# Another hand-written order of the commands in the likely branch of an attention and maxout kernel

## The chip, the core and the metric

The kernel runs on one core of a Trainium2 chip. The metric is the device time of one execution in microseconds (us). The engines are TensorE (PE in the profile; PEld is its loading of weights), VectorE (DVE), ScalarE (ACT), GpSimd (POOL) and SyncE (SP), which here only issues DMAs.

## What is computed

Attention over 4 batches, 8 heads, 768 positions and 64 features per head. A flag for each head says whether it is a retrieval head (plain causal attention) or a streaming head (causal, and only the first 4 keys and the last 64). The heads' outputs stand side by side as 3072 tokens of 512 features and go through a maxout feed-forward:

```python
scores = q @ k.T / sqrt(D)
scores = where(mask[head], scores, -1e9)   # causal, or causal & (sink | window)
a = softmax(scores)
x = (a @ v).transpose(0, 2, 1, 3).reshape(B * S, H * D)
h = maximum(maximum(x @ w1, x @ w2), x @ w3)
out = h @ w_out
```

## The kernel before

**Tiles.** A batch is cut into two halves of 384 queries; the heads are cut into two groups of four, and a group into two pairs. A "task" t counts batch, half and group: t = 4b + 2·half + group. The feed-forward runs over one half of a batch at a time, in 21 units: 18 maxout units (one of the three weights, one of six blocks of 128 hidden features; four matmuls of 384 columns) and 3 output units (128 tokens, six matmuls of 512 columns against `woutt`). There are eight such halves, and the units run strictly in that order.

**A program of commands.** The schedule is manual: the program order of the instructions on each engine is the order in which commands of a written list are executed when the kernel is built. Each engine works its own instructions off in that order and waits on semaphores where data or a buffer is missing. The flags are read at run time. A first list, FIRST, is common; then the kernel branches: the list NEAR runs where the flags have the pattern that the kernel expects (they have here), ANY otherwise; a last list, REST, is common again, behind two units that are computed ahead. The commands, with a letter at the end for the engine of the copy (d VectorE, a ScalarE, p GpSimd):

- `f 1 e`: the next unit of the feed-forward (L648 matmuls, evicted at L668 and L673; output units L692, evicted at L698 and written by SP at L699). The letter decides only for copies; the maximum is always VectorE's.
- `s t u`: unit u of the scores of task t (matmuls L876), and their exponential on ScalarE (L887). For batch 0 a third number can name one pair alone.
- `k t i u e`: a mask of pair i multiplied onto the exponentials (L908, L926).
- `av t i`: the product with the values (L964), its division (L977, L979); with `D`, SP then issues a DMA that transposes the result into xT (L984), where the feed-forward reads it. Without D, `x t i e` turns it on TensorE (L998) and copies it (L1002).
- `load b g` (GpSimd issues, L389) and `turn b g i part` (VectorE, L407) bring in and transpose keys and queries of batches 1 to 3; `cast` and `turnp half pair ee` do so for batch 0 by TensorE (L362), with one letter for each of two halves.
- `load_v b half` (SP issues, L458) and `v t i e` (L734) load and cast values; for batch 0, `v` and `vp half n e` (L747, L750) put them in order by matmuls. `c` (L799) and `kc` (L784, L790) make joined values and keys, `vf` scaled ones (L762).
- `w n`: GpSimd issues the loads of a weight (L619; `w 3`, the output weights, L623). `after_w` is a small DMA on SP that reads the output weights (L418): SP's queue waits there until they have landed.
- `m`, `nm`, `on`: masks and constants; `gate`: another waiting DMA on SP.

**Buffers that couple the engines.** In PSUM there are two score tiles `st` of two banks each, and four single banks:

```python
    sps = turns("sps", 2, space=bass.MemoryType.PSUM)
    bkp = turns("bkp", 4, space=bass.MemoryType.PSUM)
    ...
        t = bkp.tile([P, 512], FP32, tag="bank", held=False)
```

Both are taken in turn, in the order of the commands. Every unit `f`, every `av`, `x`, `vp` and each of the two halves of a `turnp` takes one `bank`; a matmul into a bank waits until the engine that evicts the bank's last contents has done so.

The list NEAR begins like this:

```python
    "x 0 0 d, w 0 2 1, x 1 1 a, x 0 1 d, cast 1 2 0 d, v 3 1 d, s 2 2 0, s 2 1 0, turnp 1 3 dd",
    "f 1 d, c 0 1 0 d, s 2 1 1, vp 1 1 a, m 0, w 1, turnp 1 2 dd, k 2 0 0 d, f 1 d, turn 1 0 0 0",
```

Of the kernel before, what the change touches and what calls it, by code (L numbers as in the profile page):

```python
# [72 lines left out]
)  # L73

NEAR = (
# [40 lines left out]
)  # L116

ANY = (
# [1029 lines left out]
```

## Time and profile before

| | |
|---|---|
| median of 3 runs | 188.49 us (188.47 to 189.35) |
| the profiled execution | 188.78 us |
| its span, first to last instruction | 187.1 us |
| mean granted TensorE clock | 1.000 |
| busy: TensorE, VectorE, ScalarE, GpSimd | 180.8, 139.9, 103.5, 85.6 us |
| read from HBM, written | 25.17 MB, 6.29 MB |

Busy times are shares of the span. Matmuls are pipelined, so their records overlap: what one costs is read from the distance between the starts, not from its length. Idle time on an engine matters only where somebody that sets the end waits for it.

### The profile page before, as it was taken

Reading aid. Unit: us, or ns where it says so; the run is one execution under the profiler, and the core shown is the slowest. Engines: PE = TensorE matmul, PEld = TensorE weight load, DVE = VectorE, ACT = ScalarE, POOL = GpSimd, SP = SyncE. Lnnn points to the kernel's source line nnn. Section 1 sums busy time; section 2 is a strip of 40 time slices with the busy share of each in tenths; the row PEclk is TensorE's granted clock in tenths of the full one; section 3 lists DMA queues with packets and bytes.
Section 4 is the critical chain, followed back from the end, with each engine's and each line's share of the span. In section 5 each row is a group of like instructions: output and inputs, shape, how many; then the busy total and the mean of one; then the engine's idle time right before and its main releaser. Section 6 shows DMA issues by size and latency. Waiting matters only on the chain. (4 is left out here: it accounts for less than half of the span.)

```text
span 187.1 us, 4937 instructions
## 1 busy us (share of the span) xinstructions
PE 180.8 (97%) x1930; PEld 104.4 (56%) x1930; DVE 139.9 (75%) x297; ACT 103.5 (55%) x164; POOL 85.6 (46%) x121
## 2 busy tenths in 40 slices
PE   7989999999999999999999999999999999999992
PEld 2446546555565545574556466664665456745552
DVE  3739999899869998999998859782758258824740
ACT  4589989542676993656675737635154534123022
POOL 6259989600569897089220466079912402000000
PEclk9999999999999999999999999999999999999999
DMA  4999999996999999983999341212202310332004
GB/s 122 272 334 310 170 196 210 206 208 129 220 206 227 185 189 225 248 98 84 187 271 185 60 172 21 46 23 109 83 2 46 113 76 2 67 110 81 7 0 168
DMA packets 43180, 26.49 MB, mean 142 GB/s; under 512 B 30866, under 2 KB 38674, under 8 KB 43154
## 3 DMA queue, kind: packets, MB, share of 16 engines
q1 hardware_dynamic: 37794, 18.03, 41.1%
q0 software_dynamic: 4944, 7.87, 23.9%
q8 instruction: 15, 0.25, 0.6%
q10 hardware_dynamic: 416, 0.26, 0.4%
q14 instruction: 11, 0.09, 0.1%
HBM read 25.17 MB, written 6.29 MB: 168 GB/s over the span
## 5 line engine op out<-in xcount | busy, mean ns | idle before, releaser
L887 ACT ACTIVATE pt<-st 128x1024 f16<-128x1024 f32 (+2 forms) x72 | 62.9, 925 | 27.1 <-PE st L876 21.9
L673 DVE TENSOR_TENSOR acc<-bank,acc 128x384 f16<-128x384 f32 x45 | 24.9, 556 | 15.1 <-PE bank L648 12.5
L648 PE MATMUL bank<-xT,w2t 128*128 128x384 f16 x180 | 36.0, 326 | 0.0
L648 PE MATMUL bank<-xT,w0t 128*128 128x384 f16 x180 | 35.7, 326 | 0.0
L648 PE MATMUL bank<-xT,w1t 128*128 128x384 f16 x180 | 35.7, 326 | 0.0
L908 POOL TENSOR_TENSOR pt<-pt,NM 128x1024 f16<-128x1024 f16 (+2 forms) x14 | 26.6, 1912 | 11.3 <-ACT pt L887 10.5
L668 ACT CAST acc<-bank 128x384 f16<-128x384 f32 x33 | 15.5, 485 | 28.8 <-PE bank L648 28.5
L692 PE MATMUL bank<-woutt,hT 128*128 128x512 f16 (+1 forms) x138 | 30.7, 372 | 0.0
L673 DVE TENSOR_TENSOR hT<-bank,acc 128x384 f16<-128x384 f32 x45 | 24.5, 557 | 4.7 <-PE bank L648 2.1
L407 DVE STREAM_TRANSPOSE KQ<-kq 128x384 f32<-128x384 f32 x24 | 25.8, 1129 | 0.4 <-issue 0.4
L926 POOL TENSOR_TENSOR pt<-pt,mk 128x512 f16<-128x512 f16 (+1 forms) x12 | 12.9, 1079 | 27.2 <-ACT pt L887 26.6
L648 PEld LDWEIGHTS <-w0t 128*128 128x128 f16 x192 | 17.9, 98 | 12.8 <-issue 1.0
L648 PEld LDWEIGHTS <-w1t 128*128 128x128 f16 x192 | 17.6, 98 | 11.6 <-issue 0.3
L648 PEld LDWEIGHTS <-w2t 128*128 128x128 f16 x192 | 17.4, 98 | 11.2 <-issue 0.4
L692 PEld LDWEIGHTS <-hT 128*128 128x128 f16 x156 | 14.4, 98 | 15.4 <-issue 0.3
L964 PEld LDWEIGHTS <-pt 128*128 128x128 f16 x492 | 18.6, 97 | 4.2 <-issue 0.8
L876 PE MATMUL st<-KQ 32*128 32x128 f16 (+4 forms) x468 | 20.8, 255 | 0.0
L964 PE MATMUL bank<-va,pt 128*128 128x65 f16 x409 | 19.8, 193 | 0.0
L979 DVE TENSOR_TENSOR x<-bank,rc 128x384 f16<-128x384 f32 x32 | 17.8, 558 | 1.1
L876 PEld LDWEIGHTS <-KQ 32*128 32x128 f16 (+1 forms) x472 | 9.6, 93 | 13.0 <-issue 9.9
L698 ACT COPY ot<-bank 128x512 f32<-128x512 f32 (+1 forms) x15 | 8.5, 569 | 14.0 <-PE bank L692 12.6
L964 PE MATMUL bank<-vf,pt 128*128 128x65 f16 x83 | 9.5, 193 | 0.0
(109 smaller groups left out, 177.7 us busy)
## 6 DMA issues: line engine op xcount, KB each, us to landing
out_dram<-ot SPq DMA_DIRECT2D x23, 256.0 KB, 2.0
vs<-in_v_dram SPq DMA_DIRECT2D x18, 256.0 KB, 6.1
kq<-in_k_dram POOLq DMA_DIRECT2D x6, 288.0 KB, 6.5
kq<-in_q_dram POOLq DMA_DIRECT2D x6, 288.0 KB, 8.0
qs<-in_q_dram SPq DMA_DIRECT2D x6, 192.0 KB, 5.0
ks<-in_k_dram SPq DMA_DIRECT2D x6, 192.0 KB, 4.5
vs<-in_v_dram SPq DMA_DIRECT2D x2, 384.0 KB, 6.3
vs<-in_v_dram SPq DMA_DIRECT2D x1, 768.0 KB, 5.7
```

The lines of the kernel that those rows point to most:

```text
L407: nc.vector.transpose(out=dst.rearrange("c (p j) -> c j p", j=n)[:, j0:j1], in_=src.rearrange("c (j i) -> c j i", i=R),)
L648: nc.tensor.matmul(yy[:, 0:HALF], w_t[wi][:, ks, ni * P : (ni + 1) * P], xT[b, half, ks].rearrange("p a t -> p (a t)"), start=(ks == 0), s ...
L668: copy_out[0](out=acc[ni], in_=yy[:, 0:HALF])
L673: nc.vector.tensor_tensor(out=dst, in0=yy[:, 0:HALF], in1=acc[ni], op=ALU.max)
L692: nc.tensor.matmul(yo[:, 0:n], hT[ns][:, tb * P : (tb + 1) * P], woutt[:, ns, c : c + n], start=(ns == 0), stop=(ns == NNB - 1),)
L698: op(out=ot[:, c : c + n], in_=yo[:, 0:n])
L876: nc.tensor.matmul(sts[x][:, c0 : c0 + n * P], keys, KQ[rows, 1, t0 : t0 + n * P], start=(c0 == 0 and r == 0 and not early), stop=(b == 0 ...
L887: nc.scalar.activation(out=pts[t, i][:, u, m0:m1, 0:w], in_=sts[i, m0][:, 0:w].unsqueeze(1) if apart else sts[i][:, :, 0:w], func=AF.Exp, ...
L908: engine.tensor_tensor(out=x, in0=x, in1=m, op=ALU.mult)
L926: engine.tensor_tensor(out=x, in0=x, in1=m, op=ALU.mult)
L964: nc.tensor.matmul(o[:, qi, hl, 0 : D + 1], pt[:, u, hl, c : c + P], vv[:, 0 : D + 1], start=(idx == 0), stop=(idx == len(todo) - 1), skip ...
L979: nc.vector.tensor_tensor(out=x, in0=o[:, :, :, 0:D], in1=rc.unsqueeze(3).to_broadcast([P, HB, 2, D]), op=ALU.mult,)
```

## The change

Only the list NEAR is replaced by another one. It has the same commands as often as before, with the same tasks, pairs and units; other are their places and the letters of their engines. No function is changed. What moves, in short: at the start `turnp 1 3` comes ahead of the scores `s 2 1 0` and `s 2 2 0`, several masks, casts and copies change engines, and `s 4 0` comes ahead of `s 3 1 1` and `av 2 0`. The loads of batch 1's values (`load_v 1 0`, `load_v 1 1`) stand later in the list, the first behind the first output unit. Here is the first part, up to where batch 1's values are used; the rest is rearranged in the same way.

```diff
 NEAR = (
-    "x 0 0 d, w 0 2 1, x 1 1 a, x 0 1 d, cast 1 2 0 d, v 3 1 d, s 2 2 0, s 2 1 0, turnp 1 3 dd",
-    "f 1 d, c 0 1 0 d, s 2 1 1, vp 1 1 a, m 0, w 1, turnp 1 2 dd, k 2 0 0 d, f 1 d, turn 1 0 0 0",
-    "s 2 3 0, s 2 3 1, k 2 1 1 d, k 2 0 1 p, kc 0 1 1 p, w 2, kc 0 0 0 a, kc 0 0 1 a, k 2 1 0 d",
-    "turn 1 0 1 0, vp 1 0 a, on 0, vp 1 2 a, s 2 2 1, f 1 a, k 2 0 2 d, turn 1 0 0 1, f 1 a",
-    "f 1 a, s 3 0 1, turn 1 0 1 1, w 3, s 3 1 1, after_w, av 2 1 D, av 2 0 D, nm, f 1 d, s 4 0",
-    "kc 0 1 0 p, f 1 d, c 0 1 1 p, load_v 1 0, f 1 d, f 1 a, load 1 1, k 3 1 1 p, f 1 a, f 1 d",
-    "s 3 0 0, s 3 1 0, load_v 1 1, f 1 a, k 4 0 1 d, k 3 1 0 d, k 3 0 0 d, k 4 0 0 p, k 3 0 1 d",
-    "f 1 d, f 1 d, load_v 2 0, s 4 1, f 1 a, f 1 a, f 1 a, av 3 1, f 1 a, av 3 0, f 1 d, f 1 a",
-    "k 4 1 0 d, x 3 0 a, turn 1 1 0 1, k 4 0 2 d, turn 1 1 0 0, x 3 1 a, kc 1 1 0 a, kc 1 0 0 p",
-    "f 1 a, f 1 a, k 4 1 1 p, v 4 1 p, v 5 0 p, turn 1 1 1 1, f 1 a, turn 1 1 1 0, f 1 a, v 5 1 d",
-    "v 4 0 p, f 1 a, f 1 d, s 5 0, f 1 a, c 1 0 0 d, f 1 d, f 1 d, f 1 a, vf 4 0 p, s 5 1",
-    "av 4 1 D, f 1 a, k 5 0 1 d, av 4 0 D, f 1 a, s 6 0, k 5 1 0 d, c 1 0 1 p, f 1 d, f 1 a",
...
+    "x 0 0 d, w 0 2 1, x 1 1 d, x 0 1 d, cast 1 2 0 a, v 3 1 d, turnp 1 3 ad, m 0, s 2 1 0",
+    "s 2 2 0, k 2 0 0 d, f 1 a, vp 1 2 d, f 1 d, s 2 1 1, w 1, k 2 0 1 d, kc 0 0 1 d, s 2 3 1",
+    "turn 1 0 1 0, turnp 1 2 aa, vp 1 1 d, f 1 a, kc 0 1 0 d, k 2 1 0 p, kc 0 1 1 p, on 0, w 2",
+    "s 2 3 0, k 2 0 2 p, s 2 2 1, vp 1 0 a, f 1 a, s 3 0 1, turn 1 0 1 1, turn 1 0 0 0, k 2 1 1 d",
+    "f 1 a, w 3, turn 1 0 0 1, nm, after_w, kc 0 0 0 d, f 1 a, av 2 1 D, s 4 0, av 2 0 D",
+    "k 4 0 1 d, f 1 d, f 1 d, c 0 1 1 p, k 3 1 0 d, c 0 1 0 d, s 3 1 1, load 1 1, f 1 a, s 3 0 0",
+    "k 3 0 0 d, s 3 1 0, f 1 a, k 3 0 1 p, f 1 d, k 4 1 0 p, f 1 a, f 1 d, f 1 d, f 1 a, av 3 0",
+    "k 3 1 1 p, f 1 a, f 1 a, av 3 1, s 4 1, f 1 a, f 1 a, turn 1 1 0 1, load_v 1 0, x 3 0 a",
+    "load_v 1 1, load_v 2 0, turn 1 1 0 0, x 3 1 a, f 1 d, f 1 a, f 1 a, f 1 a, k 4 0 0 p, f 1 a",
+    "k 4 0 2 p, kc 1 0 0 a, kc 1 1 0 a, turn 1 1 1 1, turn 1 1 1 0, v 4 0 p, v 5 1 p, f 1 d",
+    "f 1 d, vf 4 0 p, s 5 0, f 1 d, f 1 d, k 5 0 0 d, f 1 d, v 4 1 a, f 1 a, s 5 1, f 1 a",
+    "k 4 1 1 p, k 5 1 0 d, f 1 a, av 4 1 D, v 5 0 p, v 7 1 a, av 4 0 D, s 6 0, f 1 d, c 1 1 0 d",
...
 )
```

56 rows, old and new, of the table NEAR are left out of this document.

## The prediction

> **What bounds the kernel now.** I read the busy shares first, then TensorE's own waits, then the start times of its matmuls, and only then the other queues at the places that the new order touches. The page's first line on the engines:
>
> ```profile
> PE 180.8 (97%) x1930; PEld 104.4 (56%) x1930; DVE 139.9 (75%) x297; ACT 103.5 (55%) x164; POOL 85.6 (46%) x121
> ```
>
> TensorE is busy for nearly the whole span, but 97% alone doesn't say whether it runs at its pace, because matmuls overlap: a maxout matmul's record is 326 ns long in the page's groups, while four of them take 0.65 us from start to start in the chain that ended last:
>
> ```profile
> 176.56 0.65 PE bank L648 x4
> 177.21 0.65 PE st L648 x4
> ```
>
> (start, length, what). The Trainium skill says the same of any trace ("Perfetto Trace Analysis", section "Identifying the Most-Contended Engine"): matmul busy time is a poor measure of the distance to the limit, because pipelined instructions look different from what they cost. By busy time one would see 187.1 - 180.8 = 6.3 us to win here; by start times it is far less. The waits of TensorE say how much:
>
> ```profile
> PE st L484 <- DVE zero L476: 1.3, 1, 1.3
> PE bank L747 <- POOL kq L730: 0.7, 1, 0.7
> PE st L648 <- PEq L1102: 0.3, 1, 0.3
> PE bank L998 <- DVE x L979: 0.3, 1, 0.3
> PE bank L362 <- POOL qn L335: 0.2, 1, 0.2
> ```
>
> (who, for whom, us in total, times, longest). Three of the five lie ahead of the branch, which the change doesn't touch; L1102 is the entry of the common end at 175.7 us. Inside the branch, 20.4 to 175.5 us, only the 0.3 us at 21.2 us are left. A maxout unit takes 0.65 us from start to start almost everywhere there. The exceptions that I find in the timeline come to about 0.9 us in all. So TensorE is the bound and waits for nobody: an order can win a few tenths of a us at most, and whatever new wait it brings is paid in full.
>
> **Why the work itself costs the same.** Both orders hold the same commands, so TensorE has the same instructions. What neighbours cost: a unit ahead of scores takes 0.745 instead of 0.65, and scores leave the array with about 0.145 us more. Scores that follow something else are entered 33 times before and 33 times after. Four pairs of AV products now stand together instead of one, which the rows price at 0.01 us each. Sum: 0 +- 0.1 us. The other engines: casts and copies that change hands give VectorE 2.2 us more over the branch, ScalarE 2.0 and GpSimd 0.4 us less (counted instructions by the mean of their rows). VectorE is nearest to being a second bound (19.05 of 20 us busy from 80 to 100 us), but up to TensorE's 100 us mark the new order has given it 5.5 us less to do than the old one. It gets the extra after 150 us, where it is idle for over a third. I take 0 for that, hidden by TensorE.
>
> **The start of the branch, which costs.** The four PSUM banks named `bank` are taken in turn: `x 1 0`, `x 0 0`, `x 1 1`, `x 0 1`, then both halves of `turnp 1 3`. The second half needs the bank of `x 0 0`, that is, VectorE's first copy of the branch.
>
> ```profile
> 20.45 0.51 PE L998 MATMUL bank<-ident,x 128*128 128x128 f16 x6
> 21.24 0.34 PE L998 MATMUL bank<-ident,x 128*128 128x128 f16 x3 [0.28 <-DVE x L979]
> 21.51 0.62 PE L876 MATMUL st<-KQ 64*128 64x384 f16 x8
> 22.07 0.52 PE L362 MATMUL bank<-ident,qn 128*128 128x128 f16 x6
> 22.43 0.81 PE L648 MATMUL bank<-xT,w0t 128*128 128x384 f16 x4
> ...
> 24.70 0.81 PE L648 MATMUL bank<-xT,w0t 128*128 128x384 f16 x4
> ```
>
> ```profile
> 21.87 0.60 DVE L1002 COPY xT<-bank 128x384 f16<-128x384 f16 x2
> ```
>
> One copy is 0.34 us, so the bank is free at 22.21. Before, two scores (21.51 to 22.07) stand between, and the second half starts at 22.24, just free. After, `turnp 1 3` follows the third `x` at once: its first half runs at 21.42, the second could start at 21.59 and must wait until 22.21 + 0.06 (the wake-up, as from 21.18 to 21.24 at `x 0 1`): **+0.68**. What VectorE does before that copy belongs to the part ahead of the branch, so it doesn't come earlier. The scores and the first unit then follow at 22.5 and 23.1 instead of 21.5 and 22.4. Bounds: 0.5 to 0.8.
>
> The old order has a wait of its own that goes: after `turnp 1 2` (24.16, six transposes at 0.36) the unit at 24.70 waits 0.18 us for a bank that VectorE empties at 24.65. In the new order a `vp` stands there, on a bank emptied at about 25.3, against 26.1 on TensorE: **-0.18**.
>
> ScalarE takes more of the start (`cast 1 2 0`, three copies of `turnp`, two more evictions). From the late scores on, its queue is full: after the exponential of `s 2 1 1`, which ends at 26.5, come exponentials, copies and evictions of 0.74, 0.89, 0.45, 0.74, 0.96, 0.49, 0.45 and 0.96 us, so `s 3 0 1` is done at 32.2. `s 4 0` needs that tile and stands at 32.1 on TensorE, since `s 3 1 1` has been moved behind it: **+0.15** (0 to 0.4). What was there before:
>
> ```profile
> 30.69 1.58 ACT L887 ACTIVATE pt<-st 128x1024 f16<-128x1024 f32 x2
> 33.22 1.94 ACT L887 ACTIVATE pt<-st 128x1024 f16<-128x1024 f32 x2 [0.95 <-PE st L876]
> ```
>
> ScalarE was 0.95 us ahead. Sum of the start: 0.68 - 0.18 + 0.15 = +0.65 us. TensorE never idles again until 175 us, so nothing gives it back.
>
> **The transfers.** `k 2 1 0` on GpSimd now stands ahead of the weights `w 2`, and `k 2 0 2` ahead of `w 3` (the output weights). It waits for the exponential that ends at 26.5; then 1.13 + 0.42 + 0.29 + 1.96 + 1.13 us lie ahead of `w 3`: it is issued at 31.5 instead of
>
> ```profile
> 29.32 0.87 POOL L623 DMA_DIRECT2D woutt<-in_moe_w_out_dram  x1
> ```
>
> SP's queue stands still until these weights land (`after_w`), and everything behind it moves along:
>
> ```profile
> 40.09 0.76 SPq L418 DMA_DIRECT2D after<-woutt  x1
> 40.97 2.73 SPq L984 DMA_TRANSPOSE xT<-x  x2
> 43.74 10.40 SPq L458 DMA_DIRECT2D vs<-in_v_dram  x9
> ```
>
> With the same 10.8 us from issue to landing, the weights land at 42.3 instead of 40.1. From there to the landing of the second transpose the trace has 4.7 us (44.79): 47.0. The first unit of batch 0's second half reads it; it started at 46.87 and has the same TensorE work ahead of it in both orders, so 47.5. Spare: 0.5 us; cost 0. The DMA engines are busy all through 23 to 42 us (nines on the page), so the landing may be set by the traffic and not by the issue: `w 2` landed at 35.8 and the output weights 4.3 us later. The Trainium skill's "DMA: Bandwidth & Descriptors", section "Queues, rings and completion order", says that on each DMA engine descriptors are consumed in ring order; by that rule a later issue into a ring that is still full costs nothing, and the landing would stay near 40.1.
>
> The values of batch 1 now also stand behind the first output tile on SP: its unit starts at 42.65 + 0.65, and with 1.46 of matmuls, 0.59 of copy and the issue that is 45.8 instead of 43.74. The first cast on them started at 49.87; now 51.9. GpSimd's two casts, scaling and mask behind that (0.49 + 0.49 + 0.29 + 0.67) end at 53.9. `av 4 1`, started at 54.06 and moved two units back, wants them at 54.06 + 1.30 + 0.65 = 56.0. Spare 2.1; cost 0. If the cover goes, each us late is a us of TensorE.
>
> **Sum.** The profiled execution took 188.78 us, 1.68 more than its span, and 0.29 more than the median of 188.49. Span 187.1 + 0.65 = 187.75, execution 189.4, and on the median's scale 188.49 + 0.65 = **189.15**, say 189.2. 0.5% (0.94 us) is about what a measurement of this kernel can tell from no change.
>
> **Rivals.**
> *The output weights land late (slower).* If the later issue meets other traffic and they land after 42.8, SP's chain of 4.7 us comes after TensorE's 47.5 and each us beyond is lost. For it: the spare is 0.5, and the GpSimd-issued loads of this trace took 4.7 to 10.8 us to land. Against: the DMA engines are busy from 23 to 42 us, so the traffic may set the landing. Price: 1.5 us late gives 188.49 + 0.65 + 1.5 = 190.6. I give this or a like delay of a transfer 0.38.
> *Nothing is lost (no change).* The new wait at 22 us is eaten by ScalarE's and VectorE's queues, and the new order spares what is left of TensorE's small waits after 25 us, 0.2 us: 188.3 to 188.7. For it: VectorE is less pressed up to 100 us. Against: a bound engine keeps what it loses. 0.13.
> *The issue hardly moves.* SP waits until 40 us in any case, so "eight to twelve units later" in the list may be some 2 us on the chip and cost nothing; that is inside the forecast.
> *Faster by over 0.5%.* It needs 0.94 us of TensorE's waits inside the branch to go; nearly all that I found would have to, and 0.43 of it (21.2 us) is fixed by work ahead of the branch. 0.04.
>
> **The numbers.** Forecast 0.45, its own range 188.9 to 189.6; so a few of its hundredths lie over the bound of 189.43. No change within 0.5%: 0.54; slower 0.42; faster 0.04. Range 188.2 to 190.9: it takes in the no-change rival and the late weights up to 1.75 us.
>
> **What would show it.** Right: transposes at L362 idle by about 0.65 us near 21.6 with VectorE's L1002 as releaser, the first L648 at 23.1, L692's first matmul near 43.3, no wait of TensorE after 33 us. The L418 row on SP then starts at 40 to 42.5. Wrong: that idle time missing, or a wait of L648 for L984 near 47.5, of L964 near 56, or a span over 188.7.

## The result, and the profile after

The changed kernel took 190.27 us (median of 21 runs, 188.97 to 192.54), the kernel before 189.29 us beside it. The ratio is 1.0048, with a 95% interval of 1.0025 to 1.0071: 0.5 to 1.3 us slower, most likely 0.9. The forecast was +0.65 us on a median of 188.49. Later runs of the kernel before had medians of 188.5 to 188.9 us, so below everything is told as a ratio to the runs of the kernel before on the same chip, or from one profiled execution. Executions over 1.5% longer than the fastest of the same kernel are left out of the ratios.

The profiled execution of the changed kernel took 189.44 us with a span of 187.4 us. Its line of busy shares says nothing, just as before:

```profile
PE 180.9 (97%) x1930; PEld 104.9 (56%) x1930; DVE 139.7 (75%) x297; ACT 101.2 (54%) x159; POOL 85.0 (45%) x126
```

TensorE's own waits (who, for whom, us in total, times, longest) say more:

```profile
PE st L484 <- DVE zero L476: 1.3, 1, 1.3
PE bank L362 <- ACT kn L335: 0.6, 1, 0.6
PE st L648 <- PEq L1102: 0.4, 1, 0.4
PE bank L362 <- DVE xT L1002: 0.3, 1, 0.3
PE bank L998 <- DVE x L979: 0.3, 1, 0.3
```

`L362 <- DVE xT L1002` is the new wait that was predicted. The first two lines lie ahead of the branch, in code that is the same. The start of the branch, from TensorE's timeline:

```profile
20.18 0.51 PE L998 MATMUL bank<-ident,x 128*128 128x128 f16 x6
20.96 0.34 PE L998 MATMUL bank<-ident,x 128*128 128x128 f16 x3 [0.28 <-DVE x L979]
21.14 0.33 PE L362 MATMUL bank<-ident,qn 128*128 128x128 f16 x3
21.76 0.33 PE L362 MATMUL bank<-ident,qn 128*128 128x128 f16 x3 [0.29 <-DVE xT L1002]
22.02 0.61 PE L876 MATMUL st<-KQ 64*128 64x384 f16 x8
22.56 0.82 PE L648 MATMUL bank<-xT,w0t 128*128 128x384 f16 x4
...
27.99 1.10 PE L648 MATMUL bank<-xT,w0t 128*128 128x384 f16 x4
29.02 0.23 PE L876 MATMUL st<-KQ 64*128 64x128 f16 x2
...
29.35 0.50 PE L648 MATMUL bank<-xT,w0t 128*128 128x384 f16 x2
```

In the kernel before, the third to fifth unit stand in one row (x12, so the fourth starts at 28.27 and the fifth at 28.92):

```profile
27.61 2.12 PE L648 MATMUL bank<-xT,w0t 128*128 128x384 f16 x12
```

The changed kernel once more (e9 below), where nothing waited for `w 0`:

```profile
27.65 0.81 PE L648 MATMUL bank<-xT,w0t 128*128 128x384 f16 x4
...
28.86 0.99 PE L648 MATMUL bank<-xT,w0t 128*128 128x384 f16 x5
```

Three things are to be seen. The halves of `turnp 1 3` start 0.62 us apart instead of 0.17, so 0.45 us are lost (the bracket shows only 0.29, since it counts from the end of the last record). The unit at 27.99, the fourth, lasts 1.10 us instead of 0.81: its second matmul waits for the second half of `w 0`, which landed at 28.30. By starts the wait costs less: the fifth unit follows 1.36 us after the fourth, and 1.21 us in e9, so 0.15 us are lost. In the kernel before the same weights landed at 27.91 and the same unit began at 28.27, 0.36 us behind them. That wait was in no step of the prediction. Counted from `x 0 0` the fourth unit stands at 7.81 us in both orders; it is the landing that came later, 8.13 us instead of 7.46. The first half of `w 0`, issued ahead of the branch, also came close: it landed at 22.53, 0.03 us ahead of the first unit, against 21.63 and 22.43 before.

Where the time went can be added up from starts of matmuls. All profiled executions begin the branch at another time (`x 0 0` starts at 19.8 to 21.1 us, for the same code ahead of it), so I count from there. The first column is `x 0 0` to the fifth unit. The new order has `s 3 0 1` ahead of that unit and the old one behind it, so its 0.33 us are moved from the first column to the second for the new order:

| us | start | fifth to last unit of the branch | last unit to the common end | common end | sum |
|---|---|---|---|---|---|
| before | 8.46 | 144.42 | 2.41 | 11.31 | 166.60 |
| after | 8.85 | 144.48 | 2.52 | 11.34 | 167.19 |
| after, second profile (e9 below) | 8.69 | 144.48 | 2.59 | 11.34 | 167.10 |

So 0.5 to 0.6 us are in the trace: 0.2 to 0.4 at the start, 0.06 in 144 us of rearranged work, 0.1 to 0.2 at the entry to the common end, where TensorE waits for its sequencer (`PEq L1102`, 0.3 us before and 0.4 to 0.5 after). The third column is 2.41 us in all six traces that end in the old order and 2.52 or 2.59 in all eight that end in the new one. The rest is outside the span: the execution took 2.04 us more than its span, where the kernel before took 1.68 more. The medians say the same: time less span is 2.02 us over the 18 runs of the changed kernel that are kept, and 1.73 to 1.77 in the three sets of the kernel before: +0.25 us. On one chip, beside each other (e9), it is 1.98 and 1.77. Together 0.75 to 0.85 us, against 0.9 measured.

The transfers, on SP:

```profile
40.89 0.77 SPq L418 DMA_DIRECT2D after<-woutt  x1
41.77 2.75 SPq L984 DMA_TRANSPOSE xT<-x  x2
44.98 0.38 SPq L699 DMA_DIRECT2D out_dram<-ot  x1
45.41 2.48 SPq L458 DMA_DIRECT2D vs<-in_v_dram  x3
```

The output weights landed at 40.87, and the values of batch 1 went out behind the first output tile at 45.41, both close to what was worked out, and nobody waited for them.

### The profile page after: what moved, and what is told of

Read it like the earlier page. It is cut to its first block, busy times and chain, and to the rows that moved or that the text cites. A ratio compares the mean times of both kernels' runs of the same rounds, so it can differ in the third digit from the quotient of the medians.

```text
span 187.4 us, 4947 instructions
## 1 busy us (share of the span) xinstructions
PE 180.9 (97%) x1930; PEld 104.9 (56%) x1930; DVE 139.7 (75%) x297; ACT 101.2 (54%) x159; POOL 85.0 (45%) x126
## 5 line engine op out<-in xcount | busy, mean ns | idle before, releaser
L908 POOL TENSOR_TENSOR pt<-pt,NM 128x1024 f16<-128x1024 f16 (+2 forms) x11 | 19.9, 1816 | 17.9 <-ACT pt L887 15.4
L668 ACT CAST acc<-bank 128x384 f16<-128x384 f32 x26 | 12.7, 495 | 21.1 <-PE bank L648 15.1
L926 POOL TENSOR_TENSOR pt<-pt,base 128x512 f16<-128x512 f16 (+1 forms) x9 | 8.6, 954 | 26.1 <-ACT pt L887 19.9
L964 PEld LDWEIGHTS <-pt 128*128 128x128 f16 x492 | 18.2, 97 | 3.5 <-issue 0.4
L964 PE MATMUL bank<-va,pt 128*128 128x65 f16 x409 | 19.3, 193 | 0.0
L926 POOL TENSOR_TENSOR pt<-pt,mk 128x512 f16<-128x512 f16 (+1 forms) x13 | 14.0, 1082 | 6.4 <-ACT pt L887 6.2
```

The lines of the kernel that those rows point to most:

```text
L668: copy_out[0](out=acc[ni], in_=yy[:, 0:HALF])
L908: engine.tensor_tensor(out=x, in0=x, in1=m, op=ALU.mult)
L926: engine.tensor_tensor(out=x, in0=x, in1=m, op=ALU.mult)
L964: nc.tensor.matmul(o[:, qi, hl, 0 : D + 1], pt[:, u, hl, c : c + P], vv[:, 0 : D + 1], start=(idx == 0), stop=(idx == len(todo) - 1), skip ...
```

## The experiments

Twelve more sets of runs were taken, each against the kernel before on the same chip; e9 is the changed kernel again. "Old" and "new" are the two orders.

**e1: the scores back in their old place** (new order)

```diff
- v 3 1 d, turnp 1 3 ad, m 0, s 2 1 0, s 2 2 0, k 2 0 0 d
+ v 3 1 d, s 2 1 0, s 2 2 0, turnp 1 3 ad, m 0, k 2 0 0 d
```

> Theory A (the new wait of TensorE at the start is the cost: the second half of turnp 1 3 waits for VectorE's copy of x 0 0, and TensorE never idles later to give it back): the wait at L362 released by L1002 is gone, and of the 0.9 us that the new order costs about 0.45 go, the amount by which the start grew in the profiled executions; 0.3 to 0.6 us over the kernel before is left. Theory B (weights and values issued later make TensorE wait in many executions): nothing of that is touched, 0.7 to 1.0 us over the kernel before stay, whatever the wait at L362 does. Theory C (the orders are equal, and the difference is scatter): within 0.4 us of the kernel before.

Measured: 1.0049 (1.0019 to 1.0080), 0.9 us, as much as the whole change. That looks like a verdict against theory A, but the edit brought other waits. The one profiled execution (192.68 us, so long that the ratio leaves it out) has no wait at L362 for L1002, and these instead:

```profile
PE bank L648 <- DMA w0t<-in_moe_w_dram: 1.7, 2, 1.4
...
PE bank L648 <- DMA xT<-x: 0.6, 1, 0.6
```

The first unit now started at 22.09, ahead of the last part of the first half of `w 0` (22.56), and lost 0.3 us to it; the fourth lost 1.4 us to the second half, which landed at 29.83. So the second unit came 4.02 us after `x 0 0`, where the changed kernel takes 3.70. Whether the other executions waited in the same way isn't known. e1 therefore doesn't tell what the new wait alone costs.

**e2: the same wait put into the old order**

```diff
- v 3 1 d, s 2 2 0, s 2 1 0, turnp 1 3 dd, f 1 d
+ v 3 1 d, turnp 1 3 dd, s 2 2 0, s 2 1 0, f 1 d
```

> The one edit in the kernel before. Theory A: TensorE waits 0.4 to 0.7 us at L362 for L1002 near 21.6 us, and the time is 0.4 to 0.7 us over the kernel before. Theory B: the wait may show, but the time stays within 0.2 us of the kernel before, because the transfers behind are the same. Theory C: within 0.4 us.

Measured: 1.0009 (0.9979 to 1.0039), so -0.4 to +0.7 us. The wait is there:

```profile
PE bank L362 <- DVE xT L1002: 0.3, 1, 0.3
...
PE bank L648 <- DVE hT L673: 0.2, 1, 0.2
```

and the start takes 9.01 us instead of 8.46: 0.45 of it between the halves of `turnp 1 3`, 0.10 between the fourth and the fifth unit. (The second line is a wait at 79 us, for VectorE.) The time doesn't show the 0.55 us, but its interval doesn't exclude them either.

**e3: the old start, the new order behind it** (the old list up to its second unit, then the commands left, in the new order)

```diff
  ... w 1, turnp 1 2 dd, k 2 0 0 d, f 1 d
- turn 1 0 0 0, s 2 3 0, s 2 3 1, k 2 1 1 d, ...
+ vp 1 2 d, k 2 0 1 d, kc 0 0 1 d, s 2 3 1, turn 1 0 1 0, f 1 a, ...
```

> The order of before up to its second maxout unit (about 25.5 us), the new order for all that is left. Theory A: the time of before, plus 0 to 0.3 us. Theory B: 0.6 to 1.0 us over the kernel before, as all later transfers stand as in the changed kernel. Theory C: within 0.4 us.

Measured: 1.0163 (1.0130 to 1.0196), +3.1 us; no theory had that. The seam made waits of its own. TensorE's list:

```profile
PE bank L648 <- DMA xT<-x: 2.0, 1, 2.0
PE st L484 <- DVE zero L476: 1.3, 1, 1.3
PE bank L964 <- DVE pt L926: 1.0, 1, 1.0
PE bank L648 <- DVE KQ L378: 0.7, 1, 0.7
```

The lines at L964 (31 us) and L378 (26 us) lie close behind the seam. The first does not: it is the first unit of batch 2 at 112.54, which waits for transposes that SP issued at 104.93 and 106.78 and that landed at 112.19 and 112.50. This gave the next theory, D.

**e4: the new start, the old order behind it** (cut at the second unit)

```diff
  ... k 2 0 0 d, f 1 a, vp 1 2 d, f 1 d
- s 2 1 1, w 1, k 2 0 1 d, kc 0 0 1 d, ...
+ c 0 1 0 d, s 2 1 1, vp 1 1 a, w 1, turnp 1 2 dd, ...
```

> The new order up to its second maxout unit, the order of before for the rest, so the weights w 2 and w 3 and the values of batch 1 are issued as in the kernel before. Theory A: 0.4 to 0.9 us over the kernel before, as much as the whole change. Theory B: within 0.3 us of the kernel before. Theory C: within 0.4 us.

Measured: 0.9999 (0.9966 to 1.0032). The start took 8.99 us, with 0.66 us lost between the halves of `turnp 1 3`, and everything behind it is as in the kernel before, to 0.1 us. That points to the part of the new order behind its second unit, but doesn't prove it: the interval goes up to +0.6 us, and that of the changed kernel begins at +0.5. With e2: the new wait alone costs 0.5 us in the trace and at most 0.6 to 0.7 us in the time, and I take it as a part.

**e5 to e7: transposes and the load next to them.** In the new order `load 3 1` is issued at 98.7 us instead of 87.8, and SP's last transposes ahead of batch 2 go out among its traffic. SP from 96 to 110 us, after and then before:

```profile
95.88 11.43 SPq L984 DMA_TRANSPOSE xT<-x  x4
107.40 2.26 SPq L699 DMA_DIRECT2D out_dram<-ot  x3
```

```profile
95.56 1.19 SPq L984 DMA_TRANSPOSE xT<-x  x1
96.80 3.31 SPq L458 DMA_DIRECT2D vs<-in_v_dram  x3
100.22 5.06 SPq L984 DMA_TRANSPOSE xT<-x  x2
```

After, the last one lands at 108.41, and the first unit of batch 2 starts at 109.07: 0.66 us of spare (how long the data had been there when the unit came). Before: 106.39 and 108.91, 2.5 us.

e5, in the new order:

```diff
- f 1 d, av 8 1 D, s 9 1, ... s 10 1, f 1 d, load 3 1, v 13 1 a
+ f 1 d, load 3 1, av 8 1 D, s 9 1, ... s 10 1, f 1 d, v 13 1 a
```

e6, in the new order:

```diff
- s 10 1, f 1 d, load 3 1, v 13 1 a, f 1 d, v 13 0 p, av 9 1 D, av 8 0 D, f 1 a
+ s 10 1, av 9 1 D, av 8 0 D, f 1 d, load 3 1, v 13 1 a, f 1 d, v 13 0 p, f 1 a
```

e7, in the old order:

```diff
- on 1, load 3 1, av 8 0 D, ... v 13 0 p, av 9 1 D, f 1 a
+ on 1, av 8 0 D, ... v 13 0 p, av 9 1 D, load 3 1, f 1 a
```

> The changed kernel with one command moved: load 3 1 (keys and queries of batch 3's second half, GpSimd's queue) ahead of av 8 1 D, so issued near 90 us instead of 98.7 (87.8 in the kernel before). Theory D (late transposes: the last two transposes of batch 2's first half go out on SP behind the traffic of load 3 1, land 0.66 us ahead of the first unit that reads them where the kernel before has 2.5 us, and in a part of the executions TensorE waits 1 to 2 us there): they land by 107.5, the spare grows to over 1.5 us, the executions near 189 us of span go, and the time falls by 0.5 to 0.9 us against the changed kernel, to 0 to 0.4 us over the kernel before. Theory W (the fourth unit waits for the second half of w 0 near 28 us, which this doesn't touch): 0.7 to 1.0 us over the kernel before stay.

> The changed kernel with av 9 1 and av 8 0 two units earlier, ahead of load 3 1, which keeps its place. Theory D: the two transposes are issued about 1.3 us earlier and ahead of most of the load's traffic, they land by 107, the spare is 1.5 to 2.5 us, and the time falls to 0 to 0.4 us over the kernel before. Theory W: 0.7 to 1.0 us over the kernel before stay. Should VectorE or the masks not have the probabilities ready two units earlier, TensorE waits at L964 near 101 us, and 0.3 to 0.6 us are lost.

> The kernel before with the one edit in the other direction: load 3 1 moved behind av 9 1 D, to about 98 us. Theory D: the transposes of av 9 1 and av 9 0 meet its traffic, their spare falls from 2.5 us to under 1 us, and the time is 0.3 to 0.9 us over the kernel before, with some executions 1 to 2 us longer. Theory W: within 0.2 us of the kernel before.

Measured: e5 1.0073 (1.0044 to 1.0102), e6 1.0095 (1.0063 to 1.0128), e7 1.0014 (0.9987 to 1.0040). The edits widened the spare, in e5 as meant (107.43 to 109.31, 1.9 us), in e6 less (108.09 to 109.41, 1.3 us, where 1.5 to 2.5 were meant), and the time did not follow: theory D fails as the cause of the median. In e7 the spare stayed at 2.35 us, so it tells little.

**e8: the unit that reads the second half of `w 0` later** (new order)

```diff
- vp 1 0 a, f 1 a, s 3 0 1, turn 1 0 1 1
+ vp 1 0 a, s 3 0 1, f 1 a, turn 1 0 1 1
```

> The changed kernel with its fourth unit and s 3 0 1 changed over, so that the unit that reads the second half of w 0 starts 0.33 us later, at 28.3 us. Theory W: the wait of 0.28 us at L648 goes, in executions where the weights come later 0.33 us of it, and the time falls by about 0.3 us, to 0.4 to 0.7 us over the kernel before. Theory D: 0 to 0.3 us less at most, 0.6 to 1.0 us over the kernel before stay.

Measured: 1.0130 (1.0093 to 1.0166). The wait for `w 0` went as theory W had it, and a longer one came:

```profile
PE st L876 <- ACT pt L887: 0.7, 1, 0.7
...
PE bank L648 <- DMA xT<-x: 0.2, 1, 0.2
```

The score tile `st` that `s 3 0 1` writes was still being read by ScalarE's exponential; the unit that stood ahead of it had hidden that. So W was tested only with a new loss on top, and the price of the wait for `w 0` stays what the traces show. From the fourth to the fifth unit it is 0.15 us in the changed kernel, 0.2 in e5, nothing in e9 and e6, and 1.4 in the long execution of e1.

**e9: the changed kernel once more**

> The changed kernel once more, beside the others. By the profiled executions its branch start (x 0 0 to the fifth unit) is 0.4 us longer for the same work and its entry to the common end 0.1 us; theory S (that is all): 0.4 to 0.6 us over the kernel before, spans close together. Theory R (the new order also leaves the last transposes ahead of batches 1 and 2 only 0.7 us of spare, where the kernel before has 2.1 and 2.5 us, and in some executions TensorE waits 1 to 2 us there): 0.6 to 1.2 us over the kernel before, some spans 1 to 2 us above the lowest.

Measured: 1.0077 (1.0046 to 1.0108), 0.9 to 2.0 us; the middle, 1.5, is above what either theory had. Seven runs had spans from 186.9 to 188.7 us; the profiled one was the shortest, so its trace doesn't show what the others waited for. What it does show: the new wait again (0.45 us), none for `w 0`, and a late pair of transposes ahead of batch 1, landed at 68.17 with the first unit starting at 68.21. Over all traces the spare at that place is -0.5 to 2.0 us in the kernels that end in the new order (e8, where TensorE waited, is the lowest) and 1.3 to 2.35 in those that end in the old one.

**e10: the old order up to the fifth unit, then the new one**

```diff
  ... k 2 0 2 d, turn 1 0 0 1, f 1 a, f 1 a
- s 3 0 1, turn 1 0 1 1, w 3, s 3 1 1, after_w, av 2 1 D, ...
+ kc 0 1 0 d, s 3 0 1, turn 1 0 1 1, w 3, nm, after_w, f 1 a, av 2 1 D, ...
```

**e11: the new order up to the fifth unit, then the old one**

```diff
  ... s 3 0 1, turn 1 0 1 1, turn 1 0 0 0, k 2 1 1 d, f 1 a
- w 3, turn 1 0 0 1, nm, after_w, kc 0 0 0 d, f 1 a, ...
+ c 0 1 0 d, kc 0 0 0 a, turn 1 0 0 1, w 3, s 3 1 1, after_w, ...
```

> The order of before up to its fifth maxout unit (28.9 us), the new order for all that is left. Theory S: x 0 0 to the fifth unit takes 8.4 to 8.5 us again, the wait for L1002 and the one for the second half of w 0 are gone, and 0.0 to 0.3 us over the kernel before are left. Theory R: the start is as short, but the time stays 0.4 to 1.0 us over the kernel before, with spans 1 to 2 us above the lowest.

> The reverse: the new order up to its fifth maxout unit, then the order of before, so the later transfers and transposes keep the spare of before. Theory S: 0.4 to 0.6 us over the kernel before. Theory R: 0.2 to 0.5 us over the kernel before, the spans close together, the spare ahead of batches 1 and 2 at 2 us or more.

Measured: e10 1.0106 (1.0077 to 1.0134), e11 1.0054 (1.0027 to 1.0080). In e10 the start took 8.48 us, as in the kernel before, but TensorE waited elsewhere:

```profile
PE st L876 <- DVE KQ L407: 0.8, 1, 0.8
PE bank L747 <- POOL kq L730: 0.4, 1, 0.4
PE st L648 <- PEq L1102: 0.4, 1, 0.4
```

The 0.8 us (0.85 by starts) lie at 31 us, where the new order's scores came on keys that VectorE had not yet transposed; I put that down to the seam. Another 0.2 us by starts went at 109.6 us, where the first unit of batch 2 began 0.04 us after its last transpose landed (this row is not in the list, for the gap between two records was short). Without these two and the entry, its trace would be 0.2 us above the kernel before. The median of +2.0 us is above even the trace's +1.4 together with the 0.25 us outside the span. In e11 the start is the new one (9.24 us, 8.91 without `s 3 0 1`), and TensorE waits 0.32 us for a mask at 31.8 us and 0.37 us at 79 us for VectorE; time less span is 1.73 us, as in the kernel before. Neither theory S nor R took these seams into account, and the two runs don't decide between them. The start of e10 was mended and a loss stayed, where S had 0.0 to 0.3 us; but over 1 us of it is the two waits, so this doesn't rule S out.

**e12: one idea of the new order alone** (old order)

```diff
- s 2 1 1, vp 1 1 a, m 0, w 1, turnp 1 2 dd, k 2 0 0 d, f 1 d
+ s 2 1 1, m 0, w 1, turnp 1 2 dd, vp 1 1 a, k 2 0 0 d, f 1 d
```

> The kernel before with one idea of the new order alone: vp 1 1 moved behind turnp 1 2, so that the second unit doesn't wait 0.21 us for VectorE's bank. All theories: that wait goes, x 0 0 to the fifth unit takes 8.25 us instead of 8.46, and the time is 0.2 us under the kernel before, if no copy of vp 1 1 now holds a bank that the next unit wants.

Measured: 1.0040 (1.0013 to 1.0068). The wait ahead of the second unit went, and the `vp` took it over: 0.29 us for VectorE's copy of a `turnp`. The start took 8.58 us instead of 8.46, so this idea gains nothing. The time is 0.2 to 1.3 us longer, of which the trace shows 0.16 and time less span 0.05; the rest isn't explained. No kernel of these beat the kernel before, and none of the runs pointed to one that would.

## Why the prediction was right, point by point

*TensorE is the bound, and a new wait is paid in full.* Right in the traces. From the fifth unit to the last one both orders take 144.4 to 144.5 us, and the same stretch is 144.4 in e4 and e7. What a kernel lost at the start was still missing at the end of its trace: in e4 0.53 us at the start, 0.49 at the end. The time of e4 doesn't show it.

*The work costs the same (0 +- 0.1).* Right: +0.06.

*The wait at `turnp 1 3` (+0.68, bounds 0.5 to 0.8).* Right in place and releaser, too large here: 0.45 in both profiles of the changed kernel and in e8, 0.55 in e5, but 0.66 to 0.68 in e4, e6 and e11, which all start alike. The sum's step was "what VectorE does before that copy doesn't come earlier". It does at times; what goes with it stands in the last section. The first unit started at 22.56, or 2.38 us after `x 0 0`, where 2.65 had been worked out.

*The old wait of 0.18 goes.* Right: behind `turnp 1 2` at 25.11 the `vp` starts at 25.45 without a wait.

*`s 4 0` waits for ScalarE (+0.15, 0 to 0.4).* Missed, at its lower end: it starts at 31.70 straight behind `av 2 1`. ScalarE's exponential of `s 3 0 1` was done by 31.5, not 32.2.

*The output weights.* Issued at 31.34 (31.5 forecast), landed at 40.87. With the same 10.8 us of lag it would have been 42.1, with the traffic setting it 40.1, and it came in between, 9.5 us after the issue, so neither holds alone. The second transpose landed at 45.64 (47.0 at the latest was forecast), the unit that reads it started at 47.09 without a wait. The rival that put them late, at 0.38, did not come.

*The values of batch 1.* Issued at 45.41 (45.8), first cast at 51.64 (51.9), last mask ended at 53.5 (53.9), `av 4 1` did not wait. Right.

*What was not in the sum.* First, the wait for the second half of `w 0`, 0.15 us by starts. The trace of before had its margin, 0.36 us, and I looked only at loads that the change moves. The last part of that load was issued 0.44 us later, counted from `x 0 0`, behind a pause of GpSimd, and landed 0.67 us later. But e9 has the same pause, and there it landed in time (7.38 us after `x 0 0`). Over all traces of both orders it lands 7.0 to 9.7 us after `x 0 0`, so this wait is at least in part chance and not the order's price. Second, the entry to the common end, 0.1 to 0.2 us. Third, 0.25 us outside the span, a term that I took as fixed ("1.68 more than its span"). The too large terms (0.68 and 0.15) and these three nearly balance, so the forecast of +0.65 was close to +0.9 partly by luck. And the prediction named a span over 188.7 us as a sign against it. The profiled one is 187.4, but 4 of the 18 kept runs have 188.8 to 189.3, and none of the 72 in the three later sets of the kernel before is over 188.7. So some executions of the new order seem to lose more than its trace shows.

*What stays open.* The traces account for 0.75 to 0.85 us of 0.9 in the first set of runs and for less in the second (0.7 of 0.9 to 2.0). One candidate is late transposes ahead of batch 1 and batch 2: TensorE waited for transposes in the traces of e1, e3, e8 and e10, all of which end in the new order, and in none of the six that end in the old one. e5 and e6 widened the place at batch 2 and gained nothing; the place at 68 us was not tried. The other is late weights `w 0`, which cost 1.4 us in the long execution of e1 and 0.15 here; e8 was meant to test it and didn't. The time outside the span is 1.95 to 2.04 us in e1, e5, e6, e8, e9 and e10 and 1.73 to 1.88 in e2, e4, e7, e11 and e12, so it mostly goes with the order of the later part; e3, which ends in the new order and has 1.88, is an exception. Traces that end in the new order have 4947 to 4950 instructions, the others 4936 to 4938. Whether that is why isn't shown.

## What to carry to other kernels

When the bound engine has nothing left to win, price a new order by the margins that it leaves to every buffer and transfer, those of unmoved loads included: list for each load when it lands and when it is first read, in both orders, and make a term of every margin that is smaller than what landings differ by from one execution to the next (here the margin was 0.36 us, and two profiles of one kernel differed by 0.75). A wait taken away in such a schedule often moves to the next thing that had only just been in time (e1, e8, e12), so look for what stood behind it before the edit. And compare the time outside the span as well as the span; here a quarter of the loss was there.

## What the hardware did that was not expected

VectorE's copy that frees the bank comes 0.53 to 0.84 us after the start of the two casts ahead of it, for the same instructions. VectorE before and after:

```profile
21.10 0.85 DVE L730 CAST kq<-vs 128x384 f16<-128x384 f32 x2
```

```profile
20.82 0.62 DVE L730 CAST kq<-vs 128x384 f16<-128x384 f32 x2
21.35 0.88 DVE L1002 COPY xT<-bank 128x384 f16<-128x384 f16 x3
```

GpSimd issues the second half of `w 0` at that time, before and after:

```profile
20.37 1.99 POOL L619 DMA_DIRECT2D w0t<-in_moe_w_dram  x3
```

```profile
20.13 0.78 POOL L619 DMA_DIRECT2D w0t<-in_moe_w_dram  x1
21.27 1.21 POOL L619 DMA_DIRECT2D w0t<-in_moe_w_dram  x2 [0.37 <-DMA w0t<-in_moe_w_dram]
```

Before, three issues stood back to back, and the second cast took 0.59 us; it ended 0.18 us after the end of the second issue. In e4, e6, e7 and e11 it was the same (0.53 to 0.59 us, each ending 0.18 us after that issue), and in e5 and e12 it took 0.46 and 0.53 us and ended 0.15 us after the end of the first issue. After, GpSimd paused between the first and the second issue, and the cast, which began inside the pause, took 0.35 us. So in seven traces a cast on VectorE that overlaps a DMA issue on GpSimd is 0.1 to 0.2 us longer, and with it a bank and TensorE are late; this is the 0.2 us between the two values of the new wait. It is no rule: in e1, e2, e3, e8 and e10 the second cast began inside an issue too (e1: 20.89 to 21.51, cast at 21.04) and took 0.34 to 0.35 us all the same. The Trainium skill, "SBUF — State Buffer", section "SBUF: two separate sides", says that VectorE and GpSimd share one pair of ports as an exclusive lock, which whichever starts first holds for its whole instruction; of VectorE's operations it names those in a mode that uses two ports, and those with two inputs in SBUF beside a GpSimd operation that reads SBUF. The seven traces would fit such a lock, the five don't, and no run shows in which mode the cast ran, so the cause stays open.

The bracket in the last row above shows the second surprise: the profile names the landing of an earlier transfer as what released this issue on GpSimd, 0.37 us late, and names it twice more up to 24.3 us (0.34 and 0.73 us). So by the profile a load's place in the list doesn't set its issue alone; which loads ahead of it have landed counts too.
